# Key-value sums of a linear attention kernel: the side that stands in the array is exchanged

## The chip, the cores and the metric

The program runs on one core of a Trainium2 chip. Five engines work side by side there: PE (TensorE, the matmuls, with its weight loads listed as PEld), DVE (VectorE), ACT (ScalarE), POOL (GpSimd) and SP, which issues transfers. The metric is device time in microseconds (us). A weight load puts up to 128 columns of one operand (the stationary one) into the array; a matmul then streams the other operand (the moving one) through it and adds into one of eight banks of PSUM.

## The reference, cut to what matters

Attention with feature maps, for 8 batches of 8 heads, 576 tokens, 64 values and 128 features; then two blocks of matmuls (a gated one and a spatial one, "mlp" in the kernel) on its result.

```python
proj = np.einsum('bhsd,df->bhsf', x, w_phi)              # for q and for k
proj = proj - np.max(np.abs(proj), axis=-1, keepdims=True)
phi = np.concatenate([np.exp(proj), np.exp(-proj)], axis=-1)
kv = np.einsum('bhsf,bhsd->bhfd', k_p, v)                # sums over tokens
z = np.sum(k_p, axis=2)                                  # sums over tokens
num = np.einsum('bhsf,bhfd->bhsd', q_p, kv)
den = np.einsum('bhsf,bhf->bhs', q_p, z)[..., None] + 1e-06
out = num / den
```

## The kernel before, in words

Heads go in pairs: 32 pairs, P = 0 to 31. The 576 tokens of a pair are four chunks of 128 and a rest of 64; the rests of both heads share one tile of 128 rows (k4, v4: head 0 in rows 0 to 63, head 1 in rows 64 to 127, zeros elsewhere). For each pair the kernel does, in this order:

- load_k and load_q bring in transposed keys, values and queries. Values come as rows of 132 columns: 64 of head 0, four ones, 64 of head 1 (VW is 66).
- project multiplies keys and queries with w_phi, into five banks: two for keys (one a head), two for queries, one for the rests.
- kexp takes the maximum and subtracts it on DVE, and exponentiates on ACT, once for each sign s. The mapped keys kp[hh] lie as 128 tokens by 2 signs by 4 chunks by 128 features.
- kvacc sums over tokens. Values stand in the array in tiles of 32 columns, four tiles side by side (the array's column tiles, mode "128x32"), and 256 columns of mapped keys move (both signs): 16 matmuls, after one matmul of the full array for the rests. What comes out has values on partitions and features on columns, that is kv transposed. The sums z come from matmuls with a tile of ones: for P under 5 over all chunks (16 of them), from P = 5 on over what ksum has added up on DVE before (4), and 4 more with the tiles "mine" for the rests.
- kvturn copies 384 columns out of PSUM, transposes three blocks of 128 x 128 on PE against an identity (ident, built at the start by eight small DVE operations and a transfer), and copies 384 columns out again. Now features lie on partitions.
- qmax and qexp map the queries; weigh (from P = 5 on) multiplies mapped queries with z as a scalar per partition; num multiplies mapped queries with kv, in column tiles again, into three banks: two for numerators, one for denominators. divide sends the denominators' reciprocals through DRAM and multiplies.

mlp(b) takes four pairs' results and runs matmuls of the full array with single-pass operands (gemm).

All operands of the attention part are plain fp32, and one fp32 matmul of the program stands in the trace as two matmul records with two weight loads (a transpose as one). So kvacc's 16 matmuls are 32 records.

The order is written by a planner (class Plan) when the kernel is built: each operation has a key (its place in time: at(t, AK_SUM) and the like) and a modelled duration, and each engine takes the ready operation with the lowest key, with a surcharge on PE where the tiling mode of the array would change (MODE). Buffers come from two arenas in SBUF (fa for plain fp32, ra for the matmul parts of mlp, together 28880 columns) and from the eight PSUM banks.

Of the kernel before, what the change touches and what calls it, by code (L numbers as in the profile page):

```python
# [20 lines left out]
F = 128  # L21
# [5 lines left out]
VW = D + 2  # L27
HALF = S // 2
TSPLIT = ((0, 256), (256, 320))
COLS = 28880  # L30
FA_COLS = 19152
A_LEAD, A_RATE = 1.485, 1.0
AK_LOAD, AK_PROJ, AK_ACC, AK_SUM, AK_TURN = -0.545, 0.095, 0.558, 0.308, 2.337
AQ_LOAD, AQ_MAX, AQ_EXP, AQ_NUM, AQ_HEAD, A_DIV = -0.852, 0.244, 2.2, 3.059, 1.077, 5.074
W_VAL, W_CONV, W_OUT, W_G, W_U, W_SP, W_OUT2, W_STEP, W_EYE = -1.594, -1.243, -0.852, -0.897, -0.549, -0.166, 0.037, 0.06, -1.334
M_CONV, M_VAL, M_V, M_U, M_SP, M_OUT, M_ALL = -0.203, -0.337, -0.048, 0.078, -0.002, 0.205, 57.899
LONG_W, LONG_A, LONG_M = False, False, True
WINDOW = 0.405
FA_HOLD = 2373
RA_HOLD = 6427  # L40
PA_HOLD = 0
LATER = 0.108

MODE = 0.0965
# [304 lines left out]
def attn_moe_gmlp_kernel(  # L349
# [132 lines left out]
    ident = fixed([128, 128], F32, "ident")  # L482
# [4 lines left out]
    v4 = [fixed([128, 2 * D], F32, f"v4_{i}") for i in range(3)]  # L487
    ones = fixed([128, 32], F32, "ones")
    mine = [fixed([128, 32], F32, f"mine{i}") for i in range(2)]
# [36 lines left out]
    def weights():  # L526
        def at(x):
            plan.key = x
# [9 lines left out]
        for hh in range(2):  # L538
            for r in range(2):
                fill(mine[hh][64 * r:64 * r + 64], float(r == hh))  # L540
        fill(warm, 0.0)
        for i in range(3):
            at(-2.0 if i < 2 else -1.2)
            for t in (k4[i], q4[i], v4[i]):
                for hh in range(2):
                    fill(t[64 * hh:64 * hh + 64, 64 - 64 * hh:128 - 64 * hh], 0.0)
# [4 lines left out]
        at(W_EYE)  # L551

        count, row = fa.buf(128), fa.buf(1)
        plan.add({"DVE": (0.07, 0.07, lambda: nc.vector.memset(real(count[:, 0:1]), 0.0))}, [], [count])
        n = 1
        while n < 128:
            dve("tensor_scalar", out=count[:, n:2 * n], in0=count[:, 0:n], scalar1=float(n), scalar2=None, op0=ALU.add)
            n *= 2
        dma(row, count[0:1])
        dve("tensor_scalar", out=ident, in0=count, scalar1=row, scalar2=None, op0=ALU.is_equal)  # L560
# [49 lines left out]

    def load_k(P):
# [10 lines left out]
        for hh in range(2):  # L622
            r, d = half(hh), slice((2 * VW - D) * hh, (2 * VW - D) * hh + D)
            if P < WHOLE:
                copy(kl[r, r], k[r, REM:S])
                copy(vl[r, r], vt[r, d])
# [39 lines left out]

    def kvacc(kp, kpl, v, vl, terms):

        kva = psum()
# [360 lines left out]
```

## Time and profile before

| | |
|---|---|
| time, three runs | 886.75, 889.26, 890.39 us (median 889.26) |
| profiled execution, its span | 889.0 us |
| PE busy | 848.6 us (95%) |
| DVE busy | 708.0 us (80%) |
| ACT busy | 513.9 us (58%) |
| POOL busy | 151.7 us (17%) |

Busy time is the union of an engine's instructions. A matmul record lasts longer than the array is taken by it, since records overlap; what one costs is read from the distance between starts.

### The profile page before, as it was taken

Reading aid. Unit: us, or ns where it says so; the run is one execution under the profiler, and the core shown is the slowest. Engines: PE = TensorE matmul, PEld = TensorE weight load, DVE = VectorE, ACT = ScalarE, POOL = GpSimd, SP = SyncE. Lnnn points to the kernel's source line nnn. Section 1 sums busy time; section 2 is a strip of 40 time slices with the busy share of each in tenths; the row PEclk is TensorE's granted clock in tenths of the full one; section 3 lists DMA queues with packets and bytes.
Section 4 is the critical chain, followed back from the end, with each engine's and each line's share of the span. In section 5 each row is a group of like instructions: output and inputs, shape, how many; then the busy total and the mean of one; then the engine's idle time right before and its main releaser. Section 6 shows DMA issues by size and latency. Waiting matters only on the chain.

```text
span 889.0 us, 19071 instructions
## 1 busy us (share of the span) xinstructions
PE 848.6 (95%) x7312; PEld 670.8 (75%) x7312; DVE 708.0 (80%) x1660; ACT 513.9 (58%) x1089; POOL 151.7 (17%) x127
## 2 busy tenths in 40 slices
PE   4879999999999999999999999999999999999997
PEld 2435476687877988688876887678887888789896
DVE  5998889998879885898868975988878976886541
ACT  4765666866567564665656644675556646642331
POOL 4422102322011221203011210230212210100000
PEclk8989999999999999999999999999999999999999
DMA  7553343221313123121221123120321212010001
GB/s 230 192 161 101 86 123 94 56 61 52 82 51 81 29 74 91 42 61 52 50 74 53 48 74 108 28 75 27 82 63 43 61 52 67 12 47 25 25 7 59
DMA packets 64443, 62.22 MB, mean 70 GB/s; under 512 B 26718, under 2 KB 43742, under 8 KB 64352
## 3 DMA queue, kind: packets, MB, share of 16 engines
q1 hardware_dynamic: 64352, 61.01, 24.2%
q8 instruction: 57, 0.93, 0.5%
q14 instruction: 34, 0.28, 0.1%
HBM read 50.20 MB, written 9.58 MB: 67 GB/s over the span
## 4 chain that ended last, share of the span: by engine, by line
PE 59%; DVE 21%; DMA 10%; ACT 6%; issue 3%; SPq 1%; DVEq 0%; ACTq 0%
PE bank L450 43%; DVE fa L394 18%; PE bank L463 15%; ACT fa L394 5%; DMA fa<-rden 4%; DVE ra L394 2%; DMA fa<-in_w_spT_dram 2%; DMA out_dram<-fa 2%; DMA rden<-fa 1%; SPq L439 1%; DMA fa<-in_v_dram 1%; PE bank L702 1%; DMA fa<-fa 0%; DMA fa<-in_w_in_dram 0%; ACT ra L394 0%
## 5 line engine op out<-in xcount | busy, mean ns | idle before, releaser
L394 ACT ACTIVATE fa<-fa 128x512 f32<-128x512 f32 (+3 forms) x450 | 261.7, 629 | 106.0 <-DVE fa L394 79.8
L394 ACT ACTIVATE fa<-bank 128x512 f32<-128x512 f32 (+6 forms) x378 | 155.4, 456 | 144.3 <-PE bank L450 75.2
L429 POOL PARTITION_ALL_REDUCE fa<-fa x64 | 144.4, 2297 | 456.1 <-ACT fa L394 209.0
L394 DVE TENSOR_TENSOR fa<-fa 128x2 f32<-128x2 f32 (+4 forms) x348 | 158.6, 471 | 46.5 <-DMA fa<-rden 34.4
L463 PE MATMUL bank<-fa 128*32 128x288 f32 (+2 forms) x2192 | 168.7, 407 | 6.1 <-DVE fa L394 3.3
L463 PEld LDWEIGHTS bank<-fa 128*32 128x32 f32 (+1 forms) x2192 | 77.4, 113 | 84.4 <-issue 31.7
L394 ACT ACTIVATE ra<-fa 128x256 fp32r<-128x256 f32 (+5 forms) x192 | 83.8, 461 | 85.0 <-DVE fa L394 73.8
L450 PE MATMUL bank<-wg,ra 128*128 128x512 f32 (+1 forms) x480 | 115.4, 393 | 1.1 <-ACT fa L394 1.0
L394 DVE TENSOR_TENSOR ra<-fa,ra 128x256 fp32r<-128x256 f32 (+4 forms) x224 | 106.1, 502 | 12.2 <-ACT ra L394 11.5
L450 PE MATMUL bank<-ws,ra 128*128 128x256 f32 (+1 forms) x768 | 114.4, 298 | 1.1 <-DVE fa L394 0.8
L394 DVE SCALAR_TENSOR_TENSOR fa<-fa,convw 128x576 f32<-128x576 f32 x128 | 109.2, 863 | 7.1 <-ACT fa L394 6.6
L450 PE MATMUL bank<-ra,wu 128*128 128x256 f32 (+1 forms) x768 | 110.7, 299 | 3.3 <-ACT fa L394 2.6
L450 PEld LDWEIGHTS bank<-ra,wu 128*128 128x128 f32 x768 | 104.2, 189 | 11.3 <-issue 5.5
L450 PEld LDWEIGHTS bank<-ws,ra 128*128 128x128 f32 x768 | 104.8, 189 | 7.1 <-DVE fa L394 2.8
L450 PEld LDWEIGHTS bank<-ra,wv 128*128 128x128 f32 x768 | 102.6, 189 | 6.1 <-DVE fa L394 3.0
L450 PE MATMUL bank<-ra,wv 128*128 128x256 f32 (+1 forms) x768 | 104.9, 297 | 1.2 <-DVE fa L394 1.2
L450 PEld LDWEIGHTS bank<-wg,ra 128*128 128x128 f32 (+1 forms) x480 | 83.2, 177 | 26.9 <-DVE fa L394 1.9
L450 PE MATMUL bank<-wo,ra 128*128 128x512 f32 x432 | 101.6, 391 | 0.4 <-DVE fa L394 0.4
L450 PEld LDWEIGHTS bank<-wo,ra 128*128 128x128 f32 x432 | 80.4, 188 | 19.2 <-issue 2.7
L394 DVE SCALAR_TENSOR_TENSOR fa<-fa 128x576 f32<-128x576 f32 (+4 forms) x192 | 89.2, 472 | 5.7 <-ACT fa L394 3.3
L394 DVE TENSOR_REDUCE fa<-bank 128x4 f32<-128x512 f32 (+1 forms) x96 | 51.2, 547 | 20.6 <-PE bank L463 11.2
L394 DVE TENSOR_SCALAR fa<-fa 128x512 f32<-128x512 f32 (+9 forms) x194 | 49.0, 269 | 18.9 <-ACT fa L394 10.7
(72 smaller groups left out, 631.4 us busy)
## 6 DMA issues: line engine op xcount, KB each, us to landing
fa<-rden SPq DMA_DIRECT2D x64, 144.0 KB
fa<-in_v_dram SPq DMA_DIRECT2D x32, 264.0 KB
out_dram<-fa SPq DMA_DIRECT2D x32, 256.0 KB
fa<-in_qT_dram SPq DMA_DIRECT2D x28, 256.0 KB
fa<-in_kT_dram SPq DMA_DIRECT2D x28, 256.0 KB
fa<-in_w_in_dram SPq DMA_DIRECT2D x8, 512.0 KB
fa<-in_w_val_dram SPq DMA_DIRECT2D x4, 512.0 KB
fa<-in_w_outT_dram SPq DMA_DIRECT2D x4, 512.0 KB
```

Of the source, the lines that this page charges most:

```text
L394: return lambda: getattr(engine, method)(**{k: real(v) for k, v in kw.items()})
L429: getattr(nc.gpsimd, method)(*(real(a) for a in args), **{k: real(v) for k, v in kw.items()})
L439: (nc.sync if engine == "SP" else nc.scalar).dma_start(out=real(out), in_=real(in_))
L450: nc.tensor.matmul(real(acc), lhsT=real(l), rhs=real(r), start=first and i == 0, stop=last and i == n - 1)
L463: nc.tensor.matmul(real(o), lhsT=real(l), rhs=real(r), start=first, stop=last)
L702: nc.tensor.transpose(real(tp)[:, F * s:F * s + F], real(kvT)[:, F * s:F * s + F], real(ident))
```

## The change

kvacc exchanges its operands: mapped keys stand in the array, 32 features at a time in four column tiles, and values with a column of ones beside them move (DZ = 65 columns; the fp32 rows in memory already have the ones). 64 matmuls of 65 columns and, for the rests of both heads, 8 of 130 columns do all sums: what comes out has features on partitions, and for each sign and head 64 columns of kv and one of z. So ksum, the ones and "mine" matmuls of kvacc, kvturn's transposes and its second copy, and the identity are gone; kvout copies 260 columns out of PSUM. weigh and num take their columns from the new places. v4 is two columns wider, with the ones in it.

```diff
-    def kvacc(kp, kpl, v, vl, terms):
-        kva = psum()
-        out = kva[:, 0:2 * F].rearrange("p (s f) -> p s f", s=2)
-        mms, n = [(out, vl, kpl, True, False)], len(terms[0])
-        for c in range(4):
-            for j in range(4):
-                d = 2 * VW * c + (2 * VW - D) * (j // 2) + 32 * (j % 2)
-                mms.append((out[32 * j:32 * j + 32], v[:, d:d + 32], kp[j // 2][:, :, F * c:F * c + F], False, c == 3))
-        for i in range(n + 1):
-            for j in range(4):
-                o = kva[32 * j:32 * j + 32, 2 * F:3 * F]
-                mms.append((o, ones, terms[j][i], i == 0, False) if i < n
-                           else (o, mine[j // 2], kpl[:, j % 2], False, True))
-        products((8 + 4 * 8 + 4 * (n + 1)) * F / 2400 + 0.15, mms, FULL, COLS4)
-        return kva
-
-    def ksum(kp, out):
...
-        dve("tensor_tensor", out=tv, in0=kp[:, :, 0:2 * F], in1=kp[:, :, 2 * F:4 * F], op=ALU.add)
-        dve("tensor_tensor", out=out.rearrange("p (s x) -> p s x", s=2), in0=tv[:, :, 0:F], in1=tv[:, :, F:2 * F],
-            op=ALU.add)
-
-    def kvturn(kva):
...
-        copy(kvT, kva[:, 0:3 * F])
...
-                nc.tensor.transpose(real(tp)[:, F * s:F * s + F], real(kvT)[:, F * s:F * s + F], real(ident))
...
-        copy(kv, tp[:, 0:3 * F])
+    def kvacc(kp, kpl, v, vl):
+        acc, mms = psum(), []
+        for hh in range(2):
+            for c in range(4):
+                for s in range(2):
+                    o = 2 * DZ * s + DZ * hh
+                    for j in range(4):
+                        mms.append((
+                            acc[32 * j:32 * j + 32, o:o + DZ], kp[hh][:, s, F * c + 32 * j:F * c + 32 * j + 32],
+                            v[:, 2 * VW * c:2 * VW * c + 2 * VW][:, vcols(hh)], not mms or len(mms) < 4, False,
+                        ))
+        for s in range(2):
+            for j in range(4):
+                mms.append((acc[32 * j:32 * j + 32, 2 * DZ * s:2 * DZ * s + 2 * DZ], kpl[:, s, 32 * j:32 * j + 32], vl,
+                            False, s == 1))
+        products(2 * (4 * 4 + 4) * 2 * DZ / 2400 + 0.1, mms, COLS4)
+        return acc
+
+    def kvout(acc):
+        kv = fa.buf(4 * DZ)
+        copy(kv, acc[:, 0:4 * DZ])
         return kv
...
-FA_COLS = 19152
+FA_COLS = 19392
...
-MODE = 0.0965
+MODE = 0.2273
```

The keys of the order (some thirty numbers) are set anew as well; MODE, the surcharge on a change of tiling mode, is one of them, and fa takes 240 columns from ra. What the new order is, the built programs show. Tiling modes change 153 times in PE's program before and 115 times after (from the full array to column tiles 35 and 7 times, back 38 and 28, between the full array and the two row tiles of project 55 and 43, from row tiles to column tiles 9 and 21, the rest among others).

PE, middle of the program, before: one pair's sums and another's num, with gemms of mlp ahead and behind. bank names are PSUM banks, fa, v, k, q, wphi and ones SBUF tiles; x16 is a repeat of the row.

```order
L463 MATMUL bank_68<-fa,v_1_85 128x256
L463 MATMUL bank_68<-fa 32x256 x16
L463 MATMUL bank_68<-fa,ones 32x128 x4
L463 MATMUL bank_68<-fa,mine_88 32x128 x2
L463 MATMUL bank_68<-fa,mine_89 32x128 x2
L463 MATMUL bank_67<-fa 32x288 x8
L463 MATMUL bank_69<-fa 32x288 x8
L463 MATMUL bank_70<-fa,ones 32x288 x4
```

After, in the same part of PE's program, the last rows of a project, the sums of an earlier pair and the num of a third one:

```order
L464 MATMUL bank_69<-wphi,fa 128x128
L464 MATMUL bank_70<-wphi,fa 128x128
L464 MATMUL bank_71<-fa,wphi 128x512
L464 MATMUL bank_72<-fa,wphi 128x512
L464 MATMUL bank_68<-fa 32x65 x64
L464 MATMUL bank_68<-v_0_83,fa 32x130 x8
L464 MATMUL bank_71<-fa 32x288 x8
L464 MATMUL bank_72<-fa 32x288 x8
```

The sums are 72 matmuls where there were 25, project stands right ahead of them, and num writes banks 71 and 72, into which project has put the queries just before.

DVE, between the maximum of a pair's keys and its num, before (names as above; 128x512 and 128x256 from fa to fa are ksum's two additions for each head):

```order
L394 TENSOR_REDUCE fa<-bank_69 128x4
L394 TENSOR_REDUCE fa<-bank_70 128x4
L394 TENSOR_TENSOR fa<-bank_69,fa 128x512
L394 TENSOR_TENSOR fa<-bank_70,fa 128x512
L394 TENSOR_REDUCE fa<-bank_67 128x1
L394 TENSOR_TENSOR fa<-fa 128x576
L394 TENSOR_TENSOR fa<-fa 128x512
L394 TENSOR_TENSOR fa<-bank_67,fa 128x128
L394 TENSOR_TENSOR fa<-fa 128x256
L394 TENSOR_TENSOR fa<-fa 128x512
L394 SCALAR_TENSOR_TENSOR fa<-fa 128x576
L394 TENSOR_TENSOR fa<-fa 128x256
```

After, from the same operations on:

```order
L395 TENSOR_REDUCE fa<-bank_69 128x4
L395 TENSOR_REDUCE fa<-bank_70 128x4
L395 TENSOR_TENSOR fa<-bank_69,fa 128x512
L395 TENSOR_TENSOR fa<-bank_70,fa 128x512
L395 TENSOR_REDUCE fa<-bank_67 128x1
L395 TENSOR_SCALAR fa<-bank_68 128x256
L395 TENSOR_TENSOR fa<-bank_67,fa 128x128
L395 TENSOR_TENSOR fa<-fa 128x576 x2
L395 TENSOR_SCALAR fa<-fa,convw 128x576
```

The four additions are gone; DVE goes on with other work of the pair and of mlp.

## Rows read from the trace of the kernel before

**Rows 1.** The page: span, and section 1, busy us of each engine.

```profile
span 889.0 us, 19071 instructions
...
PE 848.6 (95%) x7312; PEld 670.8 (75%) x7312; DVE 708.0 (80%) x1660; ACT 513.9 (58%) x1089; POOL 151.7 (17%) x127
```

**Rows 2.** Four stretches: length, each engine's busy time (instructions), granted clock, DMA share, GB/s.

```profile
0.00:90.00 90.00, 65.89 (x640) 37.10 (x640) 73.92 (x142) 53.74 (x124) 28.34 (x45) 0.91 0.54 171
90.00:200.00 110.00, 104.62 (x929) 77.24 (x930) 101.21 (x225) 76.27 (x158) 24.86 (x14) 1.00 0.32 84
200.00:800.00 600.00, 594.68 (x5246) 481.19 (x5245) 491.85 (x1171) 357.94 (x757) 98.53 (x68) 1.00 0.21 58
800.00:889.00 89.00, 83.39 (x502) 75.27 (x500) 41.05 (x124) 25.94 (x51) 0.00 (x0) 0.98 0.09 29
```

**Rows 3.** PE's timeline, one late pair's kvacc, then num: start, length, instruction, records.

```profile
436.03 0.60 PE L463 MATMUL bank<-fa,v 128*128 128x256 f32 x2
436.56 1.93 PE L463 MATMUL bank<-fa 128*32 128x256 f32 x32
438.31 0.40 PE L463 MATMUL bank<-fa,ones 128*32 128x128 f32 x8
438.53 0.40 PE L463 MATMUL bank<-fa,mine 128*32 128x128 f32 x8
438.75 2.12 PE L463 MATMUL bank<-fa 128*32 128x288 f32 x32
440.69 0.67 PE L463 MATMUL bank<-fa,ones 128*32 128x288 f32 x8
441.28 0.73 PE L450 MATMUL bank<-wo,ra 128*128 128x512 f32 x2
```

**Rows 4.** PE's timeline, the transposes of kvturn between two gemms.

```profile
432.95 0.49 PE L702 MATMUL bank<-ident,fa 128*128 128x128 f32 x3
433.19 0.48 PE L450 MATMUL bank<-wg,ra 128*128 128x512 f32 x1
```

**Rows 5.** PE's timeline, kvacc of a pair under 5, to num's first rows.

```profile
79.19 0.59 PE L463 MATMUL bank<-fa,v 128*128 128x256 f32 x2
79.71 1.93 PE L463 MATMUL bank<-fa 128*32 128x256 f32 x32
81.46 1.06 PE L463 MATMUL bank<-fa,ones 128*32 128x128 f32 x32
...
82.55 0.43 PE L463 MATMUL bank<-fa 128*32 128x288 f32 x4
```

**Rows 6.** PE's timeline, project: from the full array to its two row tiles.

```profile
415.04 0.39 PE L463 MATMUL bank<-q,wphi 128*128 128x128 f32 x2
415.36 1.16 PE L463 MATMUL bank<-wphi,fa 64*128 64x128 f32 x16
```

**Rows 7.** Groups, DVE's additions and ACT's copies that go: count, busy us, mean ns.

```profile
L394 DVE TENSOR_TENSOR fa<-fa 128x512 f32<-128x512 f32 x54 | 37.1, 687 | 3.1 <-ACT fa L394 3.1
L394 DVE TENSOR_TENSOR fa<-fa 128x256 f32<-128x256 f32 x54 | 22.6, 418 | 0.7 <-ACT fa L394 0.4
L394 ACT ACTIVATE fa<-bank 128x384 f32<-128x384 f32 x55 | 26.8, 491 | 18.5 <-PE bank L463 14.2 <-PE bank L702 4.2
```

**Rows 8.** Groups, stretch 436.55 to 436.60: first round of a kvacc in column tiles.

```profile
L463 PE MATMUL bank<-fa 128*32 128x256 f32 x4 | 0.4, 403 | 0.0
```

**Rows 9.** Groups, stretch 437.30 to 437.40: later rounds of the same kvacc.

```profile
L463 PE MATMUL bank<-fa 128*32 128x256 f32 x8 | 0.6, 379 | 0.0
```

**Rows 10.** PEld's timeline, stretch 436.55 to 436.62: the loads of the first two rounds.

```profile
436.56 0.16 PEld L463 LDWEIGHTS bank<-fa 128*32 128x32 f32 x8 [0.33 <-issue]
```

**Rows 11.** Groups, DVE and ACT work that empties project's banks.

```profile
L394 DVE TENSOR_REDUCE fa<-bank 128x4 f32<-128x512 f32 x64 | 42.9, 680 | 18.9 <-PE bank L463 11.2 <-DMA out_dram<-fa 6.3 <-DMA rden<-fa 1.4
L394 DVE TENSOR_TENSOR fa<-bank,fa 128x512 f32<-128x512 f32 x64 | 43.1, 683 | 0.5 <-DMA out_dram<-fa 0.2 <-PE bank L463 0.2
L394 ACT ACTIVATE fa<-bank 128x512 f32<-128x512 f32 x117 | 69.8, 598 | 91.1 <-PE bank L450 57.7 <-PE bank L463 21.3 <-DMA out_dram<-fa 7.3
```

More of the change, by code (lines that the diff above doesn't have):

```diff
@@ L27 @@
 VW = D + 2
+DZ = D + 1
 HALF = S // 2
@@ L486, in attn_moe_gmlp_kernel @@
     q4 = [fixed([128, F], F32, f"q4_{i}") for i in range(3)]
-    v4 = [fixed([128, 2 * D], F32, f"v4_{i}") for i in range(3)]
+    v4 = [fixed([128, 2 * DZ], F32, f"v4_{i}") for i in range(3)]
     ones = fixed([128, 32], F32, "ones")
-    mine = [fixed([128, 32], F32, f"mine{i}") for i in range(2)]
     s2 = fixed([128, DM], F32R, "s2")
@@ L537, in weights @@
         fill(ones, 1.0)
-        for hh in range(2):
-            for r in range(2):
-                fill(mine[hh][64 * r:64 * r + 64], float(r == hh))
         fill(warm, 0.0)
@@ L550, in weights @@
              reduce_op=bass_isa.ReduceOp.absmax)
[L551 to L560, printed above, removed]
         at(-1.1)
@@ L622, in load_k @@
         for hh in range(2):
-            r, d = half(hh), slice((2 * VW - D) * hh, (2 * VW - D) * hh + D)
+            r, d, o = half(hh), vcols(hh), slice(DZ * hh, DZ * hh + DZ)
             if P < WHOLE:
                 copy(kl[r, r], k[r, REM:S])
-                copy(vl[r, r], vt[r, d])
+                copy(vl[r, o], vt[r, d])
             else:
                 dma(kl[r, r], kT[b, hp, r, REM:S])
-                dma(vl[r, r], v1[b, REM:S, hp, d])
+                dma(vl[r, o], v1[b, REM:S, hp, d])
         return k, v, kl, vl
@@ L708, in qmax, with values, totals @@
+    def kvout(acc):
+        kv = fa.buf(4 * DZ)
+        copy(kv, acc[:, 0:4 * DZ])
+        return kv
+    def values(kv, s, hh, i):
+        o = 2 * DZ * s + DZ * hh + hh + 32 * i
+        return kv[:, o:o + 32]
+    def totals(kv, s, hh, n):
+        o = 2 * DZ * s + DZ * hh + (0 if hh else D)
+        return kv[:, o:o + n]
     def qmax(parts):
@@ L726, in weigh @@
         t = fa.buf(S)
-        z = [kv[:, 2 * F + 64 * hh + 32 * s:2 * F + 64 * hh + 32 * s + 1] for s in range(2)]
+        z = [totals(kv, s, hh, 1) for s in range(2)]
         act(t, e[0], ACTF.Copy, scale=z[0])
@@ L745, in num @@
         else:
-            z = [kv[:, 2 * F + 32 * i:2 * F + 32 * i + 32] for i in range(4)]
-            terms = [[(z[2 * hh + s], es[hh][s]) for s in range(2)] for hh in range(2)]
+            terms = [[(totals(kv, s, hh, 32), es[hh][s]) for s in range(2)] for hh in range(2)]
         n = len(terms[0])
@@ L792, in attention @@
             at(t, AK_SUM)
-            if P < EARLY:
-                terms = [[kp[j // 2][:, j % 2, F * c:F * c + F] for c in range(4)] for j in range(4)]
-            else:
-                sums = fa.buf(4 * F)
-                for hh in range(2):
-                    ksum(kp[hh], sums[:, 2 * F * hh:2 * F * hh + 2 * F])
-                terms = [[sums[:, F * j:F * j + F]] for j in range(4)]
-            kva = kvacc(kp, kpl, v, vl, terms)
+            kva = kvacc(kp, kpl, v, vl)
             at(t, AK_TURN)
-            kv = kvturn(kva)
+            kv = kvout(kva)
             es, ts = [], []
```

34 lines of the change are left out of this document (14 added, 20 removed).

## The prediction

> **What bounds the kernel now.** I read the page's busy times first: PE 848.6 of 889.0 us, DVE 708.0, ACT 513.9 [rows 1]. A share over the whole span hides stages, so the stretches come next [rows 2]. From 200 to 800 us PE is busy 594.68 of 600 at full clock (1.00) while DVE has 491.85: there PE's own work is the time. From 800 on it is 83.39 of 89. From 90 to 200 both are full, PE 104.62 and DVE 101.21 of 110. In the first 90 us, with weights and first inputs coming in, PE has 65.89 and DVE 73.92. So what the change does to PE's array counts nearly whole in 689 us, and in the other 200 together with what it does to DVE. The span (889.0) is the median (889.26) to 0.03%, so I sum against 889.0.
>
> **How a matmul in column tiles is priced.** Records come in rounds of four, one for each column tile, and the distance between rounds is the price. In [rows 3] ones and mine, four rounds of 128 columns, take 438.75 - 438.31 = 0.44 us: 110 ns a round. 256 columns: 8 rounds in 438.31 - 436.56 = 1.75, 219 ns. 288 columns: 8 rounds in 440.69 - 438.75 = 1.94, 242.5 ns. These lie on a line of 0.83 ns a column (two passes at 2.4 GHz) with 4 ns over. At 65 columns the line gives 58 ns, at 130 columns 112 ns.
>
> **The sums on PE.** New kvacc: 64 matmuls are 128 records, 32 rounds of 58 ns, and 8 of 130 columns are 4 rounds of 112 ns: 1.86 + 0.45 = 2.30 us. Old kvacc from P = 5 on: 436.03 to 438.75 = 2.72 us, of which 436.56 - 436.03 - 2 x 0.219 = 0.09 is the change of mode inside it (counted below): 2.63. The transposes: 0.24 from start to start, and the gemm behind them begins with a record of 0.48 us where [rows 4] has its weights loaded late, about 0.09 more: 0.33. Saved: 2.63 + 0.33 - 2.30 = 0.66 us a pair, times 27 = 17.8. Pairs under 5 have 82.55 - 79.19 = 3.36 [rows 5], less 0.09: saved 1.30 each, 6.5 in five.
>
> **Changes of mode.** 38 fewer of 153 (the order shows them). One costs 0.09 inside kvacc; from column tiles to the full array 441.28 - 440.69 - 2 x 0.2425 = 0.105 until the next start [rows 3]; from the full array to row tiles 415.36 - 415.04 - 2 x 0.11 = 0.10 [rows 6], and after each the first round also waits for its weights, 24 ns for 32 columns (403 against 379 [rows 8, 9]) and more for 128. Between 0.1 and 0.2 each: 3.8 to 7.6, I take 6, as most of the lost ones load 128 columns next.
>
> **DVE and ACT.** ksum's additions go: 37.1 + 22.6 = 59.7 us of DVE [rows 7], and of 64 copies of 384 columns (0.491 us on ACT [rows 7]) 32 remain with 260. From 200 us on both engines have room, and this counts for nothing, except that fewer waits end late. 27 pairs with ksum over some 800 us make about four in the stretch 90 to 200: 4 x (2 x 0.687 + 2 x 0.418) = 8.8 us of DVE's 101.
>
> **The sum.** From 200 us on: 23 pairs x 0.66 = 15.2, and 5 of the 6 for modes: 20. From 90 to 200: PE saves 4 x 0.66 + 0.5 = 3.1 and DVE 8.8; both were full, the smaller holds, and some of PE's 5.4 us of idle time goes with DVE's load: 6. First 90 us: the five pairs' 6.5, of which I count half, since PE there idles 24 us for other reasons: 3. The identity's set-up is worth nothing: PE waits for inputs then. Together 29. The order puts project, sums and num in a row and lets num take the banks of the queries; I give back 1 us for it (rival 1). 889 - 28 = 861 us.
>
> **What the trace does not show** is a round of 65 columns. Below 128 columns something other than streaming may set its pace, for loads and matmuls come twice as dense. Upper ends: a round whose loads don't hide costs 24 ns more [rows 8, 9]; a round as long as the 110 ns of the shortest one seen [rows 3] costs 52 more. A lower end is the streaming itself, 54 ns. I take 58, because at the start of a kvacc, with nothing loaded, four loads side by side delay the matmuls by 24 ns alone, all four alike (403 ns each [rows 8]), and eight loads begin and end within 0.16 us [rows 10]; 24 ns of loading fit behind 54 of streaming.
>
> Two rules of the Trainium skill speak against this. "TensorE: Matmul & The Clock Gate", Part 3, "The mechanism", says that a weight load overlaps running matmuls only where its row group differs; column tiles share all rows, so no load would hide, and the time would be rival 2's, 889. The trace disagrees: a round of 128 columns takes 110 ns [rows 3], where the line has 106 of streaming. The same page ("Wait — 56ns, not 53.3ns?") has matmuls start no closer than about 25 ns, however short; by it a round of four would take 100 ns, and the kernel about 904, rival 3 in its mildest form. The trace has four starts within 0.05 us [rows 8], though in a burst; no row shows it for long.
>
> **Rivals.**
>
> 1. *PE waits for banks.* In the new order num writes banks that project filled with queries; between them stand the sums, 2.3 us, so the bank's last write is about 2.8 us old. Emptying it takes a copy of 0.598 on ACT, and the keys' banks 0.680 + 0.683 each on DVE [rows 11]. If a queue holds another operation or two, PE waits up to 1 us at each of some 23 pairs: up to 23 us, 862 to 884. Against it: ACT is busy 357.94 of 600 us, and DVE has lost 2.2 us a pair.
>
> 2. *Loads don't hide.* 36 rounds x 24 ns x 32 pairs = 27.6 us: the gain is gone, 889.
>
> 3. *Matmuls can't come so dense* (slower). A pair's sums are 288 records (loads and matmuls) in 2.3 us, 125 per us; the densest stretch in the trace, [rows 5], has 72 matmuls (8 of them in the row left out) with 72 loads in 82.55 - 79.71 = 2.84, 51 per us. If a round can't be shorter than the 110 ns seen, 32 x 52 ns x 32 pairs = 53 us is added: 861 + 53 = 914; if PE gets no more than 51 records per us at all, a pair takes 5.6 us, and the kernel 967. The sign turns where a round takes 58 + 28 / (32 x 32) us = 85 ns. Against it: the burst of [rows 10].
>
> 4. *The change is neutral since PE isn't the bound.* It would need another engine to be full from 200 on; [rows 2] has DVE at 82% before its relief. I give it no chance of its own.
>
> **Chances.** Forecast (850 to 872): 0.70. Rival 1 (872 to 884): 0.13. Rival 2 (884 to 894): 0.06. Rival 3 (above 894): 0.11. 0.5% of 889 is 4.4 us, about what a measurement of this kernel can tell from no change. Faster 0.83, same 0.06, slower 0.11. The range 848 to 882 holds the forecast with 2 us below it for a start-up that gains in full, and most of rival 1.
>
> **What will show it.** The rounds of 65 columns: 16 matmul records in a quarter of 0.93 us each, 128 in 1.86, and the sums of a pair in 2.3 us from first start to num's first. A round near 85 ns or 110 ns is rival 2 or 3. Transposes and additions of 512 and 256 columns gone from the groups, DVE near 645 us, PE near 820. Between the sums and num an idle time of PE that ACT or DVE ends is rival 1. From 200 us on PE should stay at 99%, and the stretch 90 to 200 should be some 6 us shorter. I am wrong if the stretch from 200 on loses much more or less than 20 us.

## The result, and the profile after

The changed kernel takes 876.0 us (median of four runs, 873.2 to 878.2), beside 889.8 for the kernel before on the same chip: a ratio of 0.984 (95% interval 0.980 to 0.988). It is faster, as forecast, but by 14 us where the forecast had 28. The profiled execution has a span of 873.9 us, 15.1 under the 889.0 of before.

The page of the changed kernel, span and busy times (answers to [rows 1]):

```profile
span 873.9 us, 24436 instructions
...
PE 825.1 (94%) x10104; PEld 680.6 (78%) x10104; DVE 651.6 (75%) x1539; ACT 492.9 (56%) x1061; POOL 151.1 (17%) x123
```

PE's and DVE's busy times came out near what the prediction named (820 and 645). PE is busy 23.5 us less, and the span is 15.1 shorter. The same stretches as in [rows 2], in the changed kernel:

```profile
0.00:90.00 90.00, 60.88 (x923) 37.52 (x924) 67.67 (x131) 55.83 (x131) 27.31 (x41) 0.87 0.52 164
90.00:200.00 110.00, 105.69 (x1404) 84.36 (x1403) 99.86 (x222) 76.50 (x162) 25.34 (x14) 0.98 0.32 90
200.00:800.00 600.00, 589.74 (x7377) 497.46 (x7376) 454.59 (x1089) 340.56 (x730) 98.41 (x68) 1.00 0.22 60
800.00:873.90 73.90, 68.82 (x405) 61.30 (x403) 29.48 (x99) 20.02 (x42) 0.00 (x0) 0.98 0.08 27
```

From 200 to 800 us PE now idles 10.3 us where it idled 5.3, and in the first 90 us 29.1 where it idled 24.1. One kvacc and the num behind it, the answer to [rows 3]:

```profile
459.08 2.02 PE L464 MATMUL bank<-fa 128*32 128x65 f32 x128
460.92 0.63 PE L464 MATMUL bank<-v,fa 128*32 128x130 f32 x16
463.79 2.81 PE L464 MATMUL bank<-fa 128*32 128x288 f32 x32 [2.24 <-DVE fa L395]
```

32 rounds of 65 columns take 460.92 - 459.08 = 1.84 us, 57 ns a round; the price was 58. The sums are as short as forecast. What is new stands in the last row: num waits 2.24 us for DVE.

**An account to compare kernels by.** If every PE record is priced by the distance between starts that the traces show (57 and 111 ns a round for 65 and 130 columns, 242 for 288, 120, 147 and 228 ns for gemm's 256, 320 and 512, 0.1 to 0.26 us for a change of mode), the sum is the length of PE's program if it never waited. I call it its work, and the span less the work its waits. What PE loses where its clock is low counts as waits here, since a record then takes longer than its price. Before: work 836.2, waits 52.8. After: work 804.0, waits 69.9. So the work fell by 32.2 us (the prediction's terms: 17.8 + 6.5 + 6 = 30.3) and 17.1 came back as waits. The loosest price is that of a change of mode: with 0.1 us for each of the 38 that went, the work fell by 29 and 14 came back. The question is what these 17 us are.

PE's idle time by what ended it, in the waits view of the changed kernel, first 90 us and then 200 to 800 us (what is waited for, us in total, times, longest):

```profile
PE bank L464 <- ACT k L395: 16.0, 3, 9.8
PE bank L464 <- issue: 8.4, 4, 5.2
PE bank L464 <- ACT v L395: 4.1, 1, 4.1
...
PE bank L451 <- DVE fa L395: 4.3, 5, 1.7
PE bank L464 <- DVE fa L395: 2.2, 1, 2.2
PE bank L451 <- ACT fa L395: 1.5, 3, 0.9
PE bank L464 <- issue: 1.1, 2, 0.7
PE bank L464 <- ACT fa L395: 1.1, 2, 0.8
```

and of the kernel before, 200 to 800 us:

```profile
PE bank L450 <- ACT fa L394: 2.6, 4, 1.0
PE bank L450 <- DVE fa L394: 2.0, 5, 0.6
PE bank L450 <- DMA ra<-ra: 0.4, 1, 0.4
```

Two kinds stand out. Waits that DVE ends in the middle of the program have grown from 2.0 to 6.5 us. New are waits put down to "issue", for which the profile has no releaser: over the whole span they sum to 10.6 us in seven places; before, the view has none.

### The profile page after: what moved, and what is told of

It reads as the page before. It is cut to its first block, busy times and chain, and to the rows that moved or that the text cites. A ratio compares the mean times of both kernels' runs of the same rounds, so it can differ in the third digit from the quotient of the medians.

```text
span 873.9 us, 24436 instructions
## 1 busy us (share of the span) xinstructions
PE 825.1 (94%) x10104; PEld 680.6 (78%) x10104; DVE 651.6 (75%) x1539; ACT 492.9 (56%) x1061; POOL 151.1 (17%) x123
## 3 DMA queue, kind: packets, MB, share of 16 engines
q8 instruction: 79, 1.29, 0.6%
## 4 chain that ended last, share of the span: by engine, by line
PE 70%; DVE 10%; DMA 10%; ACT 5%; issue 3%; SPq 2%; DVEq 0%; ACTq 0%
PE bank L451 49%; PE bank L464 21%; DVE fa L395 8%; DMA fa<-rden 4%; ACT fa L395 3%; SPq L440 2%; DMA fa<-in_w_spT_dram 2%; DVE ra L395 1%; DMA rden<-fa 1%; DMA fa<-in_kT_dram 1%; DMA fa<-fa 1%; DMA k<-in_kT_dram 1%; ACT ra L395 0%; DMA v<-in_v_dram 0%; DVE ws L395 0%
## 5 line engine op out<-in xcount | busy, mean ns | idle before, releaser
L395 ACT ACTIVATE fa<-fa 128x576 f32<-128x576 f32 (+3 forms) x447 | 256.8, 625 | 84.2 <-DVE fa L395 66.7
L395 ACT ACTIVATE fa<-bank 128x512 f32<-128x512 f32 (+6 forms) x353 | 140.9, 441 | 178.1 <-PE bank L451 84.6
L464 PE MATMUL bank<-fa 128*32 128x65 f32 (+2 forms) x5264 | 170.7, 267 | 5.7 <-issue 3.2
L464 PEld LDWEIGHTS bank<-fa 128*32 128x32 f32 (+1 forms) x5264 | 112.4, 111 | 65.8 <-issue 26.2
L395 DVE TENSOR_TENSOR fa<-fa 128x2 f32<-128x2 f32 (+2 forms) x240 | 99.9, 425 | 38.2 <-DMA fa<-rden 36.3
L395 ACT ACTIVATE ra<-fa 128x256 fp32r<-128x256 f32 (+6 forms) x184 | 79.0, 461 | 81.1 <-DVE fa L395 64.0
L395 DVE TENSOR_TENSOR ra<-fa,ra 128x256 fp32r<-128x256 f32 (+4 forms) x224 | 102.7, 489 | 19.6 <-ACT ra L395 12.9
L451 PEld LDWEIGHTS bank<-ra,wu 128*128 128x128 f32 x768 | 104.0, 189 | 16.4 <-ACT fa L395 7.1
L451 PE MATMUL bank<-wg,ra 128*128 128x512 f32 (+1 forms) x480 | 116.2, 399 | 0.0
L451 PE MATMUL bank<-ws,ra 128*128 128x256 f32 (+1 forms) x768 | 113.9, 297 | 1.5 <-DVE fa L395 1.1
L451 PE MATMUL bank<-ra,wu 128*128 128x256 f32 (+1 forms) x768 | 109.1, 298 | 5.9 <-ACT fa L395 4.2
L451 PEld LDWEIGHTS bank<-ws,ra 128*128 128x128 f32 x768 | 105.4, 188 | 5.8 <-DVE fa L395 2.0
L451 PEld LDWEIGHTS bank<-ra,wv 128*128 128x128 f32 x768 | 102.2, 188 | 5.3 <-issue 2.5
L451 PEld LDWEIGHTS bank<-wg,ra 128*128 128x128 f32 (+1 forms) x480 | 85.4, 180 | 26.3 <-ACT fa L395 0.5
L451 PE MATMUL bank<-ra,wv 128*128 128x256 f32 (+1 forms) x768 | 104.8, 296 | 0.2 <-DVE fa L395 0.2
L451 PE MATMUL bank<-wo,ra 128*128 128x512 f32 x432 | 103.6, 396 | 1.3 <-DVE fa L395 1.3
L395 DVE SCALAR_TENSOR_TENSOR fa<-fa 128x576 f32<-128x576 f32 (+4 forms) x192 | 91.7, 489 | 13.7 <-ACT fa L395 12.1
L451 PEld LDWEIGHTS bank<-wo,ra 128*128 128x128 f32 x432 | 80.6, 188 | 21.3 <-DVE fa L395 1.6
L395 DVE TENSOR_SCALAR fa<-fa 128x512 f32<-128x512 f32 (+8 forms) x190 | 49.8, 277 | 17.7 <-ACT fa L395 12.9
```

The costliest lines, as they stand in the source:

```text
L395: return lambda: getattr(engine, method)(**{k: real(v) for k, v in kw.items()})
L451: nc.tensor.matmul(real(acc), lhsT=real(l), rhs=real(r), start=first and i == 0, stop=last and i == n - 1)
L464: nc.tensor.matmul(real(o), lhsT=real(l), rhs=real(r), start=first, stop=last)
```

## Experiments

All are ratios of time to the kernel before on the same chip, with their 95% interval. Work and waits are those of the one profiled execution, by the account above. That execution lies within some 2.5 us of its kernel's median, but for "before, additions left out" (3.7 us under it) and "after, additions back" (7.1 above it). "issue" is that part of the waits which the waits view puts down so.

| kernel | us | ratio | span | work | waits | issue |
|---|---|---|---|---|---|---|
| before | 889 | 1 | 889.0 | 836.2 | 52.8 | 0 |
| after | 876.0 | 0.984 (0.980 to 0.988) | 873.9 | 804.0 | 69.9 | 10.6 |
| new sums, old keys | 885.6 | 0.999 (0.997 to 1.001) | 882.9 | 810.6 | 72.3 | 5.0 |
| same, new MODE | 890.9 | 1.002 (1.000 to 1.005) | 888.3 | 804.4 | 83.9 | 7.3 |
| old sums, new keys | 911.7 | 1.029 (1.024 to 1.034) | 910.4 | 836.1 | 74.3 | 1.1 |
| after, half the sums | 857.2 | 0.965 (0.960 to 0.969) | 857.0 | 775.0 | 82.0 | 2.0 |
| after, oldest bank | 858.9 | 0.967 (0.965 to 0.970) | 856.8 | 804.0 | 52.8 | 9.3 |
| before, oldest bank | 880.8 | 0.991 (0.988 to 0.994) | 877.3 | 836.2 | 41.1 | 0 |
| after, rests not waited for | 875.3 | 0.984 (0.980 to 0.988) | 875.7 | 804.0 | 71.7 | 10.8 |
| after, additions back | 914.2 | 1.030 (1.026 to 1.034) | 919.5 | 804.0 | 115.5 | 12.7 |
| oldest bank, additions back | 888.5 | 1.000 (0.998 to 1.002) | 885.8 | 804.0 | 81.8 | 8.1 |
| before, additions left out | 885.3 | 0.996 (0.994 to 0.997) | 879.5 | 836.2 | 43.3 | 0 |
| oldest bank, 128 ahead | 855.1 | 0.963 (0.961 to 0.965) | 853.7 | 804.7 | 49.0 | 4.3 |
| oldest bank, sums split | 866.8 | 0.976 (0.974 to 0.978) | 867.1 | 805.9 | 61.2 | 5.8 |
| oldest bank, two tiles | 869.2 | 0.978 (0.977 to 0.980) | 866.9 | 813.5 | 53.4 | 0.3 |
| oldest bank, old keys | 883.1 | 0.994 (0.991 to 0.996) | 881.3 | 810.6 | 70.7 | 6.1 |
| oldest bank, half the sums | 834.4 | 0.939 (0.936 to 0.942) | 834.9 | 775.0 | 59.9 | 1.9 |
| split from pair 5, 144 ahead | 853.5 | 0.960 (0.957 to 0.962) | 854.0 | 805.2 | 48.8 | 6.2 |
| split from pair 5, 128 ahead | 853.4 | 0.960 (0.958 to 0.963) | 849.1 | 805.1 | 44.0 | 3.2 |

### Is it the new order? The sums and the keys apart

The changed kernel with the keys of before (FA_COLS stays at 19392, since the old value leaves no room):

```diff
-AK_LOAD, AK_PROJ, AK_ACC, AK_SUM, AK_TURN = -0.3642, 0.0236, 0.532, 1.1165, 2.5865
+AK_LOAD, AK_PROJ, AK_ACC, AK_SUM, AK_TURN = -0.545, 0.095, 0.558, 0.308, 2.337
...
-MODE = 0.2273
+MODE = 0.0965
```

> The new sums with the old keys of the order (only the size of fa is the new one, as the old one leaves no room). Theory A, the new order gives back what the sums save: PE's program is 24.7 us shorter than before, with 149 changes of mode where before had 153, and the waits are as before: about 864 us (860 to 868). Theory B, any faster PE runs into the other engines' chains, whatever the order: PE waits some 15 us more than before, about 877 us (873 to 882).

The same with MODE alone at its new value, 0.2273:

> As the run before, with the new surcharge on a change of tiling mode alone (117 changes, project, sums and num mostly in a row, as in the changed kernel). If that surcharge brings the waits (num comes close behind a project whose banks it takes): as the changed kernel, 874 to 878 us, slower than with the old surcharge. If the other keys bring them: 858 to 864, since 32 changes of mode at 0.1 to 0.2 us are saved. Theory B: 873 to 880.

And the kernel before with the new keys (W_EYE, which the new set lacks, stays at -1.334):

> The old sums, transposes and additions with the new keys. Theory A: the new order's waits come with it, before plus about 17 us: 900 to 908 us. Theory B: nothing but the order of a PE that is as slow as before, 885 to 893 us.

The new sums gain nothing in the old order (885.6, 890.9), and the old sums lose 23 us in the new one. None of the three times lies in a range that I had given. So the order does not take back what the sums save: the new order is worth 10 us to the new sums. Each order fits its own program, and a set of keys can't be judged apart from the work it orders.

### How much of a saving on PE arrives

The changed kernel with the sums over two of four chunks (chunks 2 and 3 are left out):

```diff
-            for c in range(4):
+            for c in range(2):
```

> The changed kernel with two of the four chunks left out of the sums (its output is not the reference's): 32 matmuls a pair fewer, 16 rounds of 57 ns, 0.91 us a pair, 29 us of PE. If PE's work is the time: 876 - 29 = 847 us. If half of any saving goes into waits, as with the change: about 861 us. If PE is no longer the bound: over 868 us.

The work falls by 29.0 us and the time by 18.8, between the expectation's cases, while the waits grow by 12. So a good third of what PE saves here does not arrive; of the change's own 32.2 us it was over half.

### Banks

The order stays word for word; only the choice among free PSUM banks differs. The kernel takes the lowest free bank from 150 us on (before that it prefers banks that have rested); this version takes the one that has been free longest, all through the program.

```diff
-        if now < SOON:
+        if self.oldest:
+            o, g = min(((i, g) for g in fit for i in range(*g)), key=lambda e: (self.since[e[0]], e[0]))
+        elif now < SOON:
...
+    pa.oldest = True
```

> The changed kernel, every engine's order word for word the same; only which PSUM bank an operation gets is different: of the free banks the one that has been free longest, all through the program. In PE's program num then comes at least 4.7 us of PE's work behind the last matmul of project in its bank (2.8 to 3.8 us before, at some 20 places), and a gemm behind a gemm 5 us or more (1.4 to 2.7 before). Theory C (rival 1 of the prediction: the waits that take back part of the gain are waits for banks): PE's idle time from 200 to 800 us falls from about 10 us to under 5, and the time from 876 to 866 to 872. Rival D (PE waits for the contents, the mapped keys, queries and weighed terms that ACT and DVE deliver, whatever the bank): 874 to 878, with the same waits at the same places.

> The kernel before with the same rule for banks (longest free first), order unchanged. Theory C: the kernel before has little idle time of PE from 200 to 800 us (about 5 us), so at most 3 us are to be had: 886 to 889. Rival D: the same, 888 to 890. If it gains as much as the changed kernel does, the rule is a gain of its own and says nothing on the change.

858.9 us: 17 less, more than the 4 to 10 of the expectation, with the same instructions in the same order. The stretch of 200 to 800 us in this version:

```profile
200.00:800.00 600.00, 597.74 (x7446) 507.12 (x7445) 457.96 (x1112) 343.07 (x734) 98.86 (x68) 1.00 0.21 59
```

PE idles 2.3 us there instead of 10.3, all of it issue waits. The wait of num at 463.79 is rival 1 as it was described, on a bank of the keys. DVE's rows of the changed kernel ahead of it (its timeline; they answer to [rows 11]):

```profile
462.29 0.65 DVE L395 TENSOR_REDUCE fa<-bank 128x4 f32<-128x512 f32 x1
...
463.04 0.69 DVE L395 TENSOR_TENSOR fa<-bank,fa 128x512 f32<-128x512 f32 x1
```

Project's last records stood from 458.12 to 459.15, but DVE came to the maximum and the subtraction that empty its key bank only at 462.29 and 463.04, behind work of mlp. PE stood idle from 461.5 on, and num started when that subtraction had ended.

The kernel before gains by the same rule, though less: 8.4 us. So part of these waits is older than the change, and the change alone can't be charged with 17. What the change added is read from the two waits columns: 69.9 - 52.8 = 17.1 with the old choice, 52.8 - 41.1 = 11.7 with the new one. So some 5 us of what the change gave back went with the choice of banks, and 12 (10 by the medians: 880.8 - 858.9 = 21.9 of the 32.2) are something else that the rule leaves in place.

The granted clock has a part in these numbers. In the stretches at 0.50 PE was busy for 23.0 us in the changed kernel and for 8.4 with the new choice; before, it was 14.9 and 6.4. At half pace (46 records of num took 5.25 us there for 2.8, see the last section) half of each is lost, so by this estimate some 7 of the 17 us that the new choice gains, and 3 of the change's 5, are clock and not idle time. One such stretch, 465.13 to 468.54, stands right behind num's wait. Over the executions of each kernel the mean granted clock is 0.979 to 0.984 in the changed kernel and 0.988 to 0.993 with the new choice.

### Instructions

What is left (11.7 us) is close to the issue waits of that version, 9.3 us, of which the kernel before has none. They stand inside a kvacc or in the num right behind it. PE's timeline of the changed kernel, with the first two of them:

```profile
31.10 0.28 PE L464 MATMUL bank<-fa 128*32 128x65 f32 x4
32.84 1.95 PE L464 MATMUL bank<-fa 128*32 128x65 f32 x122 [1.45 <-issue]
34.58 0.28 PE L464 MATMUL bank<-v,fa 128*32 128x130 f32 x2
...
34.69 0.28 PE L464 MATMUL bank<-v,fa 128*32 128x130 f32 x2
40.13 0.86 PE L464 MATMUL bank<-v,fa 128*32 128x130 f32 x10 [5.16 <-issue]
```

PE stops in the middle of a run of matmuls of one form, between two records whose operands it has been reading. My first idea was that the rests' mapped keys or values came late. This version makes the eight last matmuls read keys and values that the first ones have read already (so the sums leave out the rests); the order is held:

```diff
-                mms.append((acc[32 * j:32 * j + 32, 2 * DZ * s:2 * DZ * s + 2 * DZ], kpl[:, s, 32 * j:32 * j + 32], vl,
-                            False, s == 1))
+                mms.append((acc[32 * j:32 * j + 32, 2 * DZ * s:2 * DZ * s + 2 * DZ], kp[1][:, s, 32 * j:32 * j + 32],
+                            v[:, 0:2 * DZ], False, s == 1))
```

> The changed kernel with the order of every engine the same; the eight matmuls of 130 columns in kvacc read the second head's first chunk of mapped keys and the first values in place of the rests (so the sums leave out the rests). PE's work is the same, but kvacc no longer waits for the rests' exponentials and loads. Theory E (the sums stand so close behind project that the rests, mapped last, come late): the wait of 5.2 us at 40 us and those of 0.3 to 1.1 us at 108, 325 and 378 us go, 867 to 871. Rival (the operations behind wait instead, for ACT and DVE): 873 to 876.

Nothing changed: 875.3 us, and the wait stands where it stood:

```profile
39.42 1.14 PE L464 MATMUL bank<-fa 128*32 128x130 f32 x12 [4.62 <-issue]
```

So it isn't the rests; that theory fell. What the waits have in common shows when PE's instructions between two of them are counted. Stretches of the changed kernel from one issue wait to the next (PE's and PEld's counts in brackets):

```profile
32.83:40.12 7.29, 2.13 (x128) 1.86 (x128) 6.41 (x10) 3.48 (x10) 4.49 (x3) 0.89 0.95 304
...
324.72:378.11 53.39, 53.05 (x637) 42.93 (x636) 37.90 (x104) 32.07 (x66) 9.35 (x5) 1.00 0.26 70
```

128 matmuls and 128 loads are 256 instructions; 637 + 636 and 7 semaphore instructions of PE's program are 1280, five times 256. In every kernel of this study with the new sums, the issue waits inside a kvacc stand at the same place, the 194th instruction of a block of 256, counted from the first of PE's that the trace has. (The old sums in the new order have one issue wait in a kvacc, 1.1 us, at another place; it is not explained.) And the DMA view has a queue of its own for instructions, before and after:

```profile
q8 instruction: 57, 0.93, 0.5%
```

```profile
q8 instruction: 79, 1.29, 0.6%
```

1.29 MB in 79 packets are 16 KB each, and over 2 x 10104 instructions that is 64 bytes apiece: a packet is 256 instructions. By the packets' times in the trace of the changed kernel, where PE waited, the block's packet had started 0.2 to 2.4 us after PE entered the block ahead, took 1 us, and the block's first instruction followed 1.2 to 1.6 us behind its end: 2.6 to 4.8 us from block to block. Before, PE took 7.5 us or more for any such block. A new kvacc issues 288 in 2.28 us (126 per us), and where a block falls wholly or mostly into it, PE ran dry here for up to 1.5 us. The wait of 5.16 us has a second cause beside it: the packet that ended it went out only at 37.65, 4.8 us after its block was due to be asked for, while the weights kept the DMA engines busy (share 0.95 in the row above). That the weights held it up is argued from this row, not tried.

The Trainium skill has this mechanism: "Runtime: NRT & Kernel Launch", section "Instruction fetch mechanics", tells of blocks of 256 instructions, the next fetched while the current one is executed, and calls the cost of crossing into the next mostly hidden. The block size is what the trace shows; hidden it is not here, as the row at 40.13 says.

**Moved.** If this is right, the waits follow the count and not the matmul. 32 small matmuls (128 instructions) on a tile of ones, ahead of the first project, where PE has nothing to do, on top of the oldest-bank version:

```diff
+        first = [(rest[0:32, 0:32], ones, ones, True, True)] * (32 if not xt and not began else 0)
+        began.append(1)
-        products(2 * 4 * F / 2400 + 2 * 4 * 4 * F / 4800 + 2 * 4 * REM / 4800 + 0.08, [
+        products(2 * 4 * F / 2400 + 2 * 4 * 4 * F / 4800 + 2 * 4 * REM / 4800 + 0.08, first + [
```

> The changed kernel with the bank that has been free longest, and 32 matmuls of 32 columns (128 instructions) ahead of the first project, on a tile of ones, while PE has nothing to do; every later instruction stands 128 further on. Theory F: the waits inside kvacc at 105, 318 and 372 us, all at instruction 194 or 195 of a block of 256, go; others come, again at 194 or 195, now at other matmuls; in sum much the same, 854 to 861, the less the earlier the block at 38 us is fetched. Rival (waits for data): the same waits at the same matmuls, now at instruction 66 of a block.

855.1 us. The waits at 318 and 372 us are gone, and others stand in kvaccs that had none, for instance here:

```profile
506.79 1.08 PE L468 MATMUL bank<-fa 128*32 128x65 f32 x62
508.66 0.56 PE L468 MATMUL bank<-fa 128*32 128x65 f32 x25 [0.79 <-issue]
...
707.80 1.07 PE L468 MATMUL bank<-fa 128*32 128x65 f32 x61
710.19 0.32 PE L468 MATMUL bank<-fa 128*32 128x65 f32 x7 [1.32 <-issue]
```

All six issue waits of this run are at the 194th instruction of a block again. The rival, waits for data, is refuted by this run; the one before it ruled out the rests alone. The long wait near 40 us fell to 0.6 us, and with it the issue waits from 9.3 to 4.3 us. The time fell by 3.8, so a microsecond of issue waits was worth some 0.8 of time here.

**Spread.** kvacc as two operations, the second (128 instructions less, with a later key) behind num or a project:

```diff
-        products(2 * (4 * 4 + 4) * 2 * DZ / 2400 + 0.1, mms, COLS4)
+        products(2 * 4 * 4 * DZ / 2400 + 0.07, mms[0:32], COLS4)
+        plan.key += 0.2 / 8 * A_RATE
+        products(2 * (4 * 4 * DZ + 4 * 2 * DZ) / 2400 + 0.07, mms[32:], COLS4, also=[acc])
```

> The changed kernel with the bank that has been free longest (858.9 us), and kvacc as two operations of 128 and 160 instructions (first head; second head and rests), the second with a later key, so that other work of PE mostly stands between them; the planner orders anew (127 changes of mode for 115). Theory F (instructions come late: PE's queue 8 brings 16 KB, 256 instructions, at a time; the trace shows a block start no sooner than 1.3 us after its fetch ends, and the fetch begin when the block ahead is entered, so 256 instructions in 2 us of kvacc run dry): the waits inside kvacc that nothing in the profile releases go, but for one or two of them, from about 12 us in all to under 5; 2 us more for modes: 850 to 855. Rival (those waits are for data after all): they stay, 859 to 863.

The issue waits from 90 us on all but went (0.4 us left), yet the time is 866.8, where 850 to 855 was expected. The planner's new order brought the last pair to its end later, and mlp of the last batch waits for it:

```profile
785.80 0.68 ACT L399 ACTIVATE ra<-fa 128x576 fp32r<-128x576 f32 x1 [5.32 <-DVE fa L399]
...
786.53 0.80 PE L455 MATMUL bank<-ra,wv 128*128 128x256 f32 x2 [5.68 <-ACT ra L399]
```

PE idles about 7 us there, and in the first 90 us 31.4 where it idled 25.6. An experiment that has the order made anew tests the new order too.

**Fewer.** Two column tiles of 64 in place of four of 32: 144 instructions for the same columns.

> The changed kernel with the bank that has been free longest, and kvacc in two column tiles of 64 columns where it had four of 32: half the instructions (144 a pair) for the same columns streamed; the planner orders anew with 141 changes of mode, since num keeps its four tiles. Theory F: no block of 256 instructions runs dry, 12 us come back; the changes of mode cost 5 to 9 us: 853 to 858. Rival (loads of 64 columns, 135 ns against 110 in the trace, don't hide behind 54 ns of streaming): 36 rounds x 25 to 50 ns x 32 pairs more, 885 to 915.

No packet comes late any more (0.3 us of issue waits), and a round still takes 60 ns (1.92 us for 32), so loads of 64 columns hide as well. But by the account the work is 9.5 us longer: from 26 more changes of mode, and from rounds that are 3 ns longer (3 us over 32 pairs). Other waits took the place of the issue waits (ACT ends 3.6 us of one near 113 us), and the time is 869.2. The mechanism held; the forecast for the kernel, 853 to 858, didn't.

**Both.** Split for pairs 5 to 29 alone, so that the start and the end keep their order, with 36 small matmuls ahead, and then with 32:

> The changed kernel with the bank that has been free longest, kvacc as two operations for pairs 5 to 29 only (so that the first 90 us and the end keep the order of the unsplit kernel), and 36 matmuls of 32 columns ahead of the first project, where PE has nothing to do. Theory F: about 4 us of waits for instructions are left of the 7.5 that the shifted kernel had (855.1 us), at 119 changes of mode for 115, and the first 60 us stay as short as there: 849 to 853. Rival (the split costs as much in other waits as it saves, as in the kernel split throughout, 866.8): 855 to 860.

> As i1_split_shift, with 32 matmuls ahead of the first project in place of 36, so that the first blocks of instructions begin and end where they do in the shifted kernel, whose first 90 us had 6 us less of waiting (32.3 us of PE's time behind its work by then, 38.0 in i1_split_shift). Theory F: the start of the one and the middle of the other: 853.5 - 5 = 848, 846 to 851. Rival (the first 90 us hang on the DMA's order from run to run and not on where a block begins): 853 to 855.

853.5 and 853.4 us, the best of this study, 4% under the kernel before. The first lies just above its forecast (849 to 853) and the second in its rival's range. The first's middle is as hoped, a PE that idles 0.9 us from 200 to 800:

```profile
200.00:800.00 600.00, 599.10 (x7359) 509.32 (x7349) 456.65 (x1101) 353.64 (x754) 100.91 (x68) 1.00 0.22 60
```

Its start has issue waits of 5.3 us, though; the second has 1.4 there and a profiled span 4.9 us shorter, but that execution is the lowest of its five (850.9 to 855.9), the first's profile is the highest of its five (851.1 to 855.7), and the medians are alike. Whether the start depends on where a block begins stays open.

### Do the savings arrive now?

> The sums over the first two chunks and the rests alone (two chunks are left out: 16 rounds of 57 ns, 0.91 us, a pair, 29 us of PE; 160 instructions a pair for 288), with the bank that has been free longest. With the old choice of banks 19 of the 29 us came (857.2). If what kept the rest back were waits for banks and, in the full kernel, for instructions, all comes now: 858.9 - 29 - 10 = 820, 815 to 824. Rival (ACT's and DVE's own chains are nearly as long as PE's): 832 or more.

834.4 us: of the 29.0 us of work 24.5 arrive, where 18.8 did, and the waits are 59.9 beside 52.8, although the issue waits fell by 7.4. So with the new choice of banks most of a saving comes, but not all: waits that ACT and DVE end stand again where there were none, 4.8 us from 200 to 800 us. Of these, 3.3 end with an operation that reads a PSUM bank, so banks are not out of the way. The rival's 832 or more held.

> The new sums in the order that the old keys give (885.6 us with the old choice of banks), with the bank that has been free longest. If the new order owes its worth to banks alone, this comes down to the changed kernel's 859 with the same rule; by the trace 43 us of its 67 us of waits lie before 90 us, where the rule already held, so 12 to 16 us are to be had: 869 to 874.

883.1 us, 2.5 less than with the old choice of banks and not the 12 to 16 that I expected. The new order's worth is not a matter of banks: with the same rule it is 24 us ahead, 6.6 in work (34 changes of mode fewer) and 17.9 in waits, which I have not traced further.

### What DVE's relief is worth

The additions of ksum put back into the changed kernel, their results unused, at the place where kvacc is planned, once with the old and once with the new choice of banks; and left out of the kernel before, whose order stays (the matmuls with ones read one chunk instead of the sum):

```diff
+            for e in kp:
+                for n in (F, F // 2):
+                    x = real(e)[:, :, 0:2 * n]
+                    y = real(e)[:, :, 2 * n:4 * n]
+                    nc.vector.tensor_tensor(
+                        out=real(spare)[:, 0:4 * n].rearrange("p (s x) -> p s x", s=2), in0=x, in1=y, op=ALU.add
+                    )
```

> The changed kernel with the additions of the kernel before put back on DVE for pairs from 5 on (54 of 512 and 54 of 256 columns, about 60 us of DVE's time, their results unused and nobody waits for them), issued where kvacc is planned; everything else in the same order. By the prediction's steps DVE's relief is worth nothing from 200 us on and some 3 to 6 us between 90 and 200: 877 to 882. Rival (DVE's queue ends PE's waits everywhere): 2.2 us a pair come back in part at each of 27 pairs, 890 or more.

> The changed kernel with the bank that has been free longest and the additions of the kernel before put back on DVE, unplanned, their results unused (60 us of DVE's time; without the rule for banks they cost 38 us). Theory C (a late DVE reaches PE through banks that are taken again soon): 864 to 874. Rival (it reaches PE through the mapped keys and weighed queries themselves): the 38 us again, 890 to 900.

> The kernel before without ksum's additions (108 DVE operations, 60 us, left out; the matmuls with ones read the first chunk of the mapped keys instead), every engine's order else the same, PE's work the same. By the prediction's step DVE's relief is worth nothing from 200 us on and at most 6 us before: 883 to 889. Rival (a DVE that is ahead keeps PE from waiting for banks): 876 to 882.

The answers differ by direction. Left out of the old order, 60 us of DVE are worth 3.5 us. Put back into the new one without a plan for them, they cost 38 us, or 30 with the new choice of banks, where I had expected 5 to 15. That does not show that a late DVE reaches PE by another way than banks. In the run with the new choice, four additions stand for 2.33 us in DVE's queue ahead of the maximum and the subtraction that empty a project's key banks, and num's product with ones starts when the first of the two subtractions has ended:

```profile
590.41 2.33 DVE L684 TENSOR_TENSOR spare<-fa 128x512 uint8<-128x512 f32 x4
592.65 1.28 DVE L399 TENSOR_REDUCE fa<-bank 128x4 f32<-128x512 f32 x2
593.85 1.28 DVE L399 TENSOR_TENSOR fa<-bank,fa 128x512 f32<-128x512 f32 x2
...
594.58 0.69 PE L469 MATMUL bank<-fa,ones 128*32 128x288 f32 x8 [3.20 <-DVE fa L399]
```

From 90 us on ACT and DVE end 25.2 us of PE's waits in this run, and all but 0.8 end with an operation that reads a PSUM bank. So the likelier reading is that with a late DVE the longest rest which the order allows is still too short; no run here separates the bank from its contents.

An engine that is 76% busy has room for what the order has a place for, and next to none for what comes in between.

## Why the prediction was right, and where it was wrong

**Price of a round: right.** 57 ns at 65 columns and 111 at 130, against 58 and 112, and 2.28 us a pair against 2.30. Rival 2 (loads that don't hide) and rival 3 in both its forms (rounds of 110 ns, 51 records per us) fell with it. By the Trainium skill's rule on row groups ("TensorE: Matmul & The Clock Gate", Part 3, "The mechanism") the loads could not have hidden; they do, at 57 ns a round for 32 rounds.

**Work saved on PE: right.** 32.2 us by the account against 30.3 forecast. The 38 changes of mode are 7 of it, against 6.

**DVE and ACT: right in the sum.** Leaving out the additions gave 3.5 us in the old order; the prediction had up to 6, all of it before 200 us. The copy of 384 columns (491 ns) became one of 260 (383 ns):

```profile
L395 ACT ACTIVATE fa<-bank 128x260 f32<-128x260 f32 x29 | 11.1, 383 | 21.0 <-PE bank L464 21.0
```

**The give-back: wrong.** "I give back 1 us for it" is the step that failed: 17 us came back by the account. The time, 876, lies in the range that the prediction gave to rival 1 with a chance of 0.13. Three things are in it.

- Rival 1 was right in kind: PE waits for banks that DVE and ACT have yet to empty. I argued it away with ACT's busy share and DVE's lost 2.2 us a pair. Shares say nothing about a queue in a given order: at 463 us DVE was late because of what stood ahead of it. In the place that I had named, num behind project, the 2.24 us at 463.79 are the one long wait from 200 to 800 us; of the 9.1 us that DVE and ACT end there, 5.8 are gemms' (L451). With the choice of banks changed, these waits went, in both kernels; about 5 us were the change's own, clock included.
- Rival 3 asked the right question, whether matmuls can come so dense, and answered it from a burst [rows 10]. The limit is not in a round but in 256 instructions: the array takes 126 per us, and the next block is not there. The issue waits are 10.6 us, four fifths of them (8.4) in the first 90 us. That they are the larger part of the 17 is in part argued: in the first 90 us PE idles only 5.0 us more than before, and the shift took 5.0 us of such waits away for 3.8 us of time.
- The clock was not in the sum. PE was busy at half its clock for 23.0 us where it was for 14.9: some 4 us more lost, by the estimate above, and these 4 are part of what the other two gave back. A wait can cost twice: during the one that ended at 40.13 the clock fell, and PE went on at half of it.

**The first 90 us: not the 3 us that I counted.** PE idled 5 us more there, with 8.4 us of issue waits that nothing in the trace of before could show, against the 6.5 us that the sums save. mlp's first gemm starts at 108.96 us where it started at 111.31, so about 2 us were gained up to there. From 200 us to the end the span is 15.1 us shorter (689.0, now 673.9), where 20 were forecast, and PE is busy 98.3% from 200 to 800 us, where 99% were.

With the banks chosen by age the changed kernel takes 858.9 us, near the forecast's 861, but that is no vindication: the rule gives the kernel before 8.4 us too, and against that one the change is worth 21.9 us, some 10 less than the work saved, and the issue waits are 9.3.

## What to carry to other kernels

A saving on the bounding engine is a saving in its work; how much arrives depends on what ends last behind it, so price the waits of the new order by place (which bank, which queue, what stands ahead in it), not by busy shares. Give a freed bank the longest rest that the order allows: taking the bank that has been free longest cost nothing and gave 8 and 17 us (2.5 in an order that waited for other things). When an edit multiplies the instructions of an engine, count them per microsecond as well: 72 small matmuls instead of 25 large ones were faster in the array, and PE outran the fetch of its instructions.

## What the hardware showed that I had not expected

- PE's instructions arrive in packets of 256, and by the packets' times the next one is asked for about when the block ahead is entered: with 2.6 to 4.8 us from one block to the next where PE waited, 126 instructions per us can't be kept up beyond a block. In the changed kernel this made waits of 0.3 to 1.5 us, and one of 5.16 us while the weights were loading.
- During that wait PE's granted clock fell to 0.50, the lower of its two levels, and 46 records of num took 5.25 us; at the 242 ns a round of [rows 3] they take 2.8. The timeline's row, and stretches of the changed kernel with the granted clock third from the right (the last one right behind num's wait at 463.79):

```profile
40.95 5.25 PE L464 MATMUL bank<-fa 128*32 128x288 f32 x46
```

```profile
40.00:44.00 4.00, 3.87 (x42) 2.70 (x45) 0.00 (x0) 1.51 (x3) 0.00 (x0) 0.50 0.33 114
...
56.00:62.00 6.00, 5.29 (x172) 3.33 (x160) 4.56 (x8) 3.77 (x9) 4.27 (x2) 1.00 0.63 214
...
465.13:468.54 3.41, 3.41 (x28) 1.73 (x21) 3.38 (x13) 0.98 (x5) 2.18 (x2) 0.50 0.00 0
```

- Loads and matmuls of 32 columns alternate for 128 records on end at 14 ns per matmul, with four tiles side by side; two tiles of 64 columns do the same work at 60 ns a round.
